# Score products of the later twenty tiles as two 64-row products, one per head of a pair, in place of one zero-padded 128-row product

## The chip, the cores and the metric

The kernel runs on one core of one Trainium2 chip. The metric is the device time of a run in microseconds. Engines: PE is TensorE's matmul side, PEld its weight loads, DVE is VectorE, ACT is ScalarE, POOL is GpSimd, SP is SyncE, which issues the DMAs.

## The reference, cut to what matters

```
batch 4, heads 8, sequence 768, head_dim 64, d_model 512, d_ff 1536
scores = q @ k^T / 8          # mask: heads 0, 2, 6 causal; the others 4 sinks + a window of 64
a      = softmax(scores)
x      = (a @ v), heads side by side            # (3072, 512)
out    = (silu(x @ w_gate) * (x @ w_val)) @ w_out
```

The result is compared with a float32 reference; the kernel multiplies in fp16 and accumulates in fp32.

Of the kernel before, what the change touches and what calls it, by code (L numbers as in the profile page):

```python
# [9 lines left out]
AF = mybir.ActivationFunctionType  # L10
# [102 lines left out]
def kernel(  # L113
# [13 lines left out]
    nc = tc.nc  # L127
# [29 lines left out]
    scale = 1.0 / (D ** 0.5)  # L157
# [18 lines left out]
    def buf(ring, shape, dt, name):  # L176
        return pools[ring].tile(shape, dt, name=name, tag=ring)
# [23 lines left out]
    def pe(d):  # L201
# [13 lines left out]
        out=ident, in_=ident, compare_op=ALU.not_equal, fill=1.0,  # L215
# [13 lines left out]
    OWN, DIAG, FAR, BAND0 = range(4)  # L229

    m0 = const.tile([128, 8, 128], FH, name="m0")
    m1 = const.tile([128, 4, 128], FH, name="m1")
    m2 = const.tile([128, 5, 128], FH, name="m2")
# [29 lines left out]

    def mask_fill(x):
        ps = mask_ps[0]
        for dst, src in ((m2[:, 0:1], OWN), (m2[:, 1:4], DIAG), (m2[:, 4:5], FAR),
                         (m1[:, 0:2], OWN), (m1[:, 2:4], FAR),
                         (m0[:, 0:4], BAND0), (m0[:, 4:6], DIAG), (m0[:, 6:7], BAND0),
                         (m0[:, 7:8], DIAG))[5 * x:5 + 5 * x]:
            nc.vector.tensor_scalar(  # L270
                out=dst, in0=ps[:, src].unsqueeze(1).to_broadcast([128, dst.shape[1], 128]),
                scalar1=-1.0 / OFF, op0=ALU.mult, scalar2=1.0, op1=ALU.add)
# [6 lines left out]
    qT = [const.tile([128, 2, 4, 2, 128], FH, name=f"qT{n}") for n in range(2)]  # L279
# [20 lines left out]
    def warm(n=40):  # L300
# [3 lines left out]
        for _ in range(n):  # L304
# [6 lines left out]
                     after=[T_fill0]) for x in range(4)]  # L311
    T_mord = P.add("mord", [pe(0.216)], -0.5, mask_order, deps=[T_masks], takes=["tr"])
    T_fill = [P.add(f"mfill{x}", [dve(1.3 + 0.1 * x)], -0.4, (lambda x=x: mask_fill(x)),
                    deps=[T_mord]) for x in range(2)]
    P.uses(T_mord, "tr", *T_fill)
# [96 lines left out]
    LEAD = 4  # L412
# [100 lines left out]
    def plan(t):  # L513


        b, i = TILES[t]
        if i == 0:
            if t == 0:
                return [([(p, (0, 1), 2 * x, 0) for x, p in enumerate(ps)], 4, None)
                        for ps in ((2, 3), (0, 1))]  # L520
            return [([(p, (0, 1), 2 * x, 0) for x, p in enumerate((2, 3, 0, 1))], 8, m0)]
        if t == 1:
            return [([(p, (0, 1), 0, i), (p, (0, 1), 2, -1)], 4, None) for p in (2, 3)] + [
                ([(1, (0, 1), 0, i), (0, (0, 1), 2, i)], 4, None),
                ([(1, (0,), 0, -1), (1, (1,), 1, 0), (0, (0, 1), 2, 0)], 4, None)]
        us = [([(2, (0, 1), 0, i), (2, (0, 1), 2, -1), (3, (0, 1), 4, i), (3, (0, 1), 6, -1)],
               8, m1),
              ([(1, (0, 1), 0, i), (0, (0, 1), 2, i), (1, (0,), 4, -1), (1, (1,), 5, 0),
                (0, (0, 1), 6, 0)], 8, m2)]
        rest = [(0, (0, 1), kt) for kt in range(1, i)] + [(1, (1,), kt) for kt in range(1, i)]  # L530
        unit, at = [], 0
        for p, hh, kt in rest:
            if at + len(hh) > 8:
                us.append((unit, at, None))
                unit, at = [], 0
            unit.append((p, hh, at, kt))
            at += len(hh)
        if unit:
            us.append((unit, at, None))
        return us  # L540

    def marks(t, u):

        if t >= LEAD:
            return []
        if t == 0:
            return [[(0, BAND0, 4)], [(0, DIAG, 2), (2, BAND0, 1), (3, DIAG, 1)]][u]
        if t == 1:
            return [[(0, OWN, 2), (2, FAR, 2)], [(0, OWN, 2), (2, FAR, 2)],
                    [(0, OWN, 1), (1, DIAG, 3)], [(0, FAR, 1)]][u]  # L550
        if TILES[t][1] == 0:
            return [(0, BAND0, 4), (4, DIAG, 2), (6, BAND0, 1), (7, DIAG, 1)]
        if u == 0:
            return [(0, OWN, 2), (2, FAR, 2), (4, OWN, 2), (6, FAR, 2)]
        return [(0, OWN, 1), (1, DIAG, 3), (4, FAR, 1)]

    def block(t, p, kt):

        b, i = TILES[t]
        if kt < 0 and i > 1:  # L560
            return k2[b % 2][:, p, i - 2, :]
        kt = max(kt, 0)
        return kT[b % 2][:, p, kt * 128:(kt + 1) * 128]

    def value(t, h, kt):
        b, i = TILES[t]
        if kt < 0 and i > 1:
            return v2[b % 2][:, i - 2, h, 0:65]
        return vt[b % 2][:, max(kt, 0), h, 0:65]

    whole_sc, es, av_blocks = {}, {}, {}

    def score_ring(t, u):
        return "gv" if t < 2 and u % 3 else "sc"

    def scores(t, u, unit):
        if t < 2:
            sc = [buf(score_ring(t, u), [128, 4, 128], FP, "sc")]
            whole_sc[t, u] = sc[0]
        else:  # L580
            sc = whole_sc[t, u] = buf("sc", [128, 8, 128], FP, "sc")
            sc = [sc[:, 0:4], sc[:, 4:8]]
        half = slice(t % 2 * 64, t % 2 * 64 + 64)
        terms = [(c, n, perm, nat[:, m].unsqueeze(1).to_broadcast([128, n, 128]))
                 for c, m, n in marks(t, u)]
        terms += [(c, len(hh), block(t, p, kt), qT[t // 2 % 2][:, hh[0]:hh[-1] + 1, p, :, half])
                  for p, hh, c, kt in unit[0]]
        for c, n, weights, moving in terms:
            first, last = True, True
            if t < LEAD:  # L590

                in_bank = [x for x in terms if x[0] // 4 == c // 4]
                first, last = moving is in_bank[0][3], moving is in_bank[-1][3]
            nc.tensor.matmul(  # L594
                sc[c // 4][:, c % 4:c % 4 + n, :], weights, moving, start=first, stop=last)

    def exps(t, u, unit):
        e = es[t, u] = buf("e", [128, 8, 128], FH, "e")
        for p, hh, c, kt in unit[0]:
            for n, s_ in enumerate(hh):  # L600
                h = PAIRS[p][s_]
                av_blocks.setdefault((t, h), []).append((e[:, c + n, :], value(t, h, kt)))
        n = unit[1]
        nc.scalar.activation(  # L604
            out=e[:, 0:n], in_=whole_sc.pop((t, u))[:, 0:n], func=AF.Exp, scale=scale)

    def mask(task, t, u, m):
        ev, mm = es[t, u][:, 0:m.shape[1]], m
        if m is m1:
            ev = es[t, u].rearrange("p (g n) q -> p g (n q)", g=2)  # L610
            mm = m.rearrange("p n q -> p (n q)").unsqueeze(1).to_broadcast([128, 2, 512])
        ENG[task().way[0]].tensor_tensor(out=ev, in0=ev, in1=mm, op=ALU.mult)  # L612
# [162 lines left out]
    def tasks_of_tile(t):  # L775
        b, i = TILES[t]
        pos = place(t)
        units = plan(t)
        n = t // 2
        k_deps = [x for kt in range(i // 2 + 1) for x in T_ev[QP.index((b, kt)), 2]]  # L780
# [8 lines left out]
        for u, unit in enumerate(units):  # L789
            mms, nb, m = unit  # L790
            sc = P.add(f"sc{t}.{u}", [pe(sum(0.056 if len(x[1]) == 1 else 0.109 for x in mms)
                                       + sum(x[2] * 0.056 for x in marks(t, u)))],
                       pos + 0.01 * u, (lambda t=t, u=u, unit=unit: scores(t, u, unit)),
                       deps=k_deps + (pk_deps if u < 2 else []) + ([T_masks] if t < LEAD else []), takes=[score_ring(t, u)], kind="",
                       grp=f"tile{t}", after=T_seq.get("sc", []))
            T_seq["sc"] = [sc]
            sc.nmm = len(mms) + len(marks(t, u))
            T_sc_of[b, i].append(sc)
            ex = P.add(f"ex{t}.{u}", [act(128 * nb)], pos + 0.01 * u,
                       (lambda t=t, u=u, unit=unit: exps(t, u, unit)), deps=[sc], takes=["e"],  # L800
                       grp=f"tile{t}", after=T_seq.get("ex", []))
            T_seq["ex"] = [ex]
# [3 lines left out]
            if m is not None and t >= LEAD:  # L806
                cell = []
                size = m.shape[1] * 128 * (2 if m is m1 else 1)
                ways = [pool(0.16 + size * 0.00192), both(0.08 + size * 0.00062)]
                ms.append(P.add(f"mask{t}.{u}", ways, pos + 0.01 * u,  # L810
                                (lambda cell=cell, t=t, u=u, m=m:
                                 mask(lambda: cell[0], t, u, m)),
                                deps=[ex] + T_fill, grp=f"tile{t}"))
                cell.extend(ms)
# [115 lines left out]
    for g in range(NG):  # L930
# [3 lines left out]
        for j in range(NJ):  # L934
# [5 lines left out]
            for c in parts:  # L940
                n = c[1] - c[0]
                mm = 4 * (n / 2400 + 0.0025)
# [99 lines left out]
```

## The kernel before: the parts that the change touches

The work is cut into 24 tiles of 128 queries. Heads go in pairs, and since a head has 64 dimensions, the pair's two heads fill the 128 partitions of `kT`: head 0 in rows 0 to 63, head 1 in rows 64 to 127. The queries `qT` hold, for each head of the pair, a block whose other 64 rows are zero. One product of the 128-row keys with both blocks side by side (256 columns) therefore gives both heads' scores at once, half of its multiplications being by zero.

```python
PAIRS = [(0, 2), (4, 6), (1, 3), (5, 7)]
kT = [const.tile([128, 4, S], FH, name=f"kT{n}") for n in range(2)]
qT = [const.tile([128, 2, 4, 2, 128], FH, name=f"qT{n}") for n in range(2)]
...
nc.vector.memset(qT[n][0:64, 1], 0.0)       # head 1's block: rows of head 0 are zero
nc.vector.memset(qT[n][64:128, 0], 0.0)
```

A *unit* is up to eight cells of 128 keys x 128 queries: two PSUM banks of four cells. `plan` lists the units of a tile; an entry is (pair, heads, first cell, key block). A unit's scores are followed by one exponential (ACT), a mask multiplication for some (POOL or DVE), and the value products.

```python
us = [([(2, (0, 1), 0, i), (2, (0, 1), 2, -1), (3, (0, 1), 4, i), (3, (0, 1), 6, -1)], 8, m1),
      ([(1, (0, 1), 0, i), (0, (0, 1), 2, i), (1, (0,), 4, -1), (1, (1,), 5, 0),
        (0, (0, 1), 6, 0)], 8, m2)]
...   # then the older key blocks, eight cells at a time

def scores(t, u, unit):
    ...
    terms += [(c, len(hh), block(t, p, kt), qT[t // 2 % 2][:, hh[0]:hh[-1] + 1, p, :, half])
              for p, hh, c, kt in unit[0]]
    for c, n, weights, moving in terms:
        ...
        nc.tensor.matmul(sc[c // 4][:, c % 4:c % 4 + n, :], weights, moving, start=first, stop=last)
```

The order of all work on each engine is fixed by a long string that the change leaves alone.

The softmax here doesn't subtract the row's maximum and nothing guards it: scores larger than these inputs give would overflow.

## Time and profile before

| | before |
|---|---|
| median of 3 runs | 268.32 us |
| lowest to highest | 268.29 to 268.49 us |
| profiled span | 266.5 us |
| matmuls, of them score products of the 54 units that change | 1984, 230 |
| busy: PE, ACT, DVE | 95%, 64%, 64% |

The lines on which most rests are shown in the prediction. How to read them: a digit of the busy rows is the busy share of one of 40 slices, in tenths. In a table of stretches the columns after the stretch and its length are the busy microseconds of PE, PEld, DVE, ACT and POOL, with counts. In the timeline the columns are start, duration, engine, line and operation, output from inputs, and how many were merged. A matmul's record is longer than its share of a stream (272 ns against 109 between starts in the prediction's timeline), so the distance from one start to the next, called *slot* here, is taken as what it costs in a stream. One more view of before is needed for the comparison: the weight loads ahead of and within a unit, from the timeline of PEld.

```profile
198.57 0.10 PEld L875 LDWEIGHTS <-wg_sb 128*128 128x128 f16 x1
198.79 0.10 PEld L594 LDWEIGHTS <-kT 128*128 128x128 f16 x1
199.00 0.10 PEld L594 LDWEIGHTS <-k 128*128 128x128 f16 x1
```

The first product of that unit starts at 199.00 (prediction, timeline). Its weights were loaded from 198.79, while the last gate product was still streaming: **each load runs one product ahead**.

### The profile page before, as it was taken

To read this page: it belongs to the slowest core of one execution; us is meant where nothing else is said; L and a number is where in the kernel's file an instruction comes from. 1 tells how busy PE (TensorE), PEld (TensorE's weight loads), DVE (VectorE), ACT (ScalarE), POOL (GpSimd) and SP (SyncE) were. 2 spreads that over 40 slices of the span, in tenths; PEclk is the share of its full clock that TensorE was granted. 3 is DMA by queue.
4 is the path that set the end of the run, shared out by engine and by line. 5 is a ranking of instruction groups with operands and counts; after the bars stand their busy time and mean duration, and the time that the engine had idled before them with its cause. 6 is when DMAs were issued, how large, how long until landed. Compare 5 with 4: busy or idle time off the path is not lost.

```text
span 266.5 us, 5265 instructions
## 1 busy us (share of the span) xinstructions
PE 254.4 (95%) x1984; PEld 146.4 (55%) x1984; DVE 171.6 (64%) x345; ACT 171.0 (64%) x283; POOL 92.3 (35%) x126
## 2 busy tenths in 40 slices
PE   7899689999999999999999999999999999999993
PEld 7777565566555555654555555545555654444441
DVE  7665678867476886549876455578446767466332
ACT  3799999999999874895696555665443643423000
POOL 8748866445358323388003230520122020000000
PEclk9999999999999999999999999999999999999999
DMA  7999999999899939956543911551231200101134
GB/s 189 305 333 333 305 328 383 317 246 305 259 292 217 230 85 299 213 108 127 118 92 60 159 39 43 117 100 23 63 76 21 57 7 17 39 2 41 39 89 109
DMA packets 75193, 41.23 MB, mean 155 GB/s; under 512 B 27552, under 2 KB 70560, under 8 KB 75168
## 3 DMA queue, kind: packets, MB, share of 16 engines
q1 hardware_dynamic: 75088, 40.78, 61.6%
q8 instruction: 15, 0.25, 0.4%
q10 hardware_dynamic: 80, 0.13, 0.2%
q14 instruction: 10, 0.08, 0.1%
HBM read 28.31 MB, written 6.29 MB: 130 GB/s over the span
## 4 chain that ended last, share of the span: by engine, by line
PE 71%; ACT 17%; DMA 3%; SPq 3%; issue 2%; DVE 1%; ACTq 0%
PE gv L875 40%; PE o_ps L904 20%; PE sc L594 7%; ACT e L604 5%; ACT v L183 4%; PE av L624 4%; DMA raw<-in_v_dram 3%; ACT vt L183 2%; ACT hq L183 2%; SPq L330 2%; ACT sig L881 2%; SPq L338 1%; ACT k L183 1%; PE tr L472 1%; ACT wo_sb L183 0%
## 5 line engine op out<-in xcount | busy, mean ns | idle before, releaser
L604 ACT ACTIVATE e<-sc 128x1024 f16<-128x1024 f32 (+4 forms) x71 | 62.2, 880 | 26.3 <-PE sc L594 25.9
L875 PE MATMUL gv<-xt,wv_sb 128*128 128x512 f16 (+1 forms) x304 | 70.8, 368 | 1.3 <-DVE sil L885 1.3
L904 PE MATMUL o_ps<-wo_sb,h 128*128 128x512 f16 x288 | 71.2, 379 | 0.1
L875 PE MATMUL gv<-xt,wg_sb 128*128 128x512 f16 (+1 forms) x304 | 70.6, 368 | 0.6 <-DVE xt L185 0.5
L885 DVE SCALAR_TENSOR_TENSOR sil<-sig,gv 128x512 f32<-128x512 f32 (+1 forms) x76 | 49.7, 656 | 31.7 <-ACT sig L881 31.1
L881 ACT ACTIVATE sig<-gv 128x512 f32<-128x512 f32 (+1 forms) x76 | 43.3, 574 | 36.5 <-PE gv L875 36.2
L892 DVE SCALAR_TENSOR_TENSOR h<-sil,gv 128x512 f16<-128x512 f32 (+1 forms) x76 | 48.7, 654 | 7.7 <-PE gv L875 7.0
L612 POOL TENSOR_TENSOR e<-e,m 128x640 f16<-128x640 f16 (+1 forms) x16 | 27.5, 1716 | 69.4 <-ACT e L604 54.3
L875 PEld LDWEIGHTS <-wv_sb 128*128 128x128 f16 x304 | 28.9, 98 | 29.0 <-issue 2.0
L875 PEld LDWEIGHTS <-wg_sb 128*128 128x128 f16 x304 | 28.9, 98 | 27.9 <-issue 1.6
L904 PEld LDWEIGHTS <-h 128*128 128x128 f16 x288 | 26.8, 98 | 26.1 <-issue 0.5
L594 PE MATMUL sc<-qT,kT 128*128 128x256 f16 (+1 forms) x228 | 35.6, 257 | 1.3 <-ACT e L604 1.2
L594 PEld LDWEIGHTS <-kT 128*128 128x128 f16 x228 | 20.5, 98 | 12.8 <-issue 2.3
L624 PEld LDWEIGHTS <-e 128*128 128x128 f16 x472 | 20.1, 97 | 8.2 <-ACT e L604 0.9
L185 POOL COPY v<-vt 32x528 f16<-32x528 f16 (+1 forms) x36 | 22.4, 621 | 4.6 <-ACT vt L183 2.5
L185 POOL CAST vt<-raw 64x512 f16<-64x512 f32 x23 | 15.8, 689 | 20.9 <-DMA raw<-in_v_dram 16.3
L624 PE MATMUL av<-vt,e 128*128 128x65 f16 x392 | 21.8, 193 | 0.5 <-ACT e L604 0.4
L641 DVE TENSOR_TENSOR xb<-av,rc 128x256 f16<-128x256 f32 x47 | 19.8, 424 | 1.6
L629 DVE RECIPROCAL rc<-av 128x4 f32<-128x4 f32 x48 | 8.5, 178 | 19.0 <-PE av L624 18.7
L183 ACT CAST hq<-raw 128x512 f16<-128x512 f32 x28 | 16.9, 617 | 4.4 <-DMA raw<-in_q_dram 3.6
L185 DVE COPY o_sb<-o_ps 128x512 f32<-128x512 f32 x14 | 9.6, 688 | 14.4 <-PE o_ps L904 14.4
L612 DVE TENSOR_TENSOR e<-e,m 128x1024 f16<-128x1024 f16 (+1 forms) x22 | 14.7, 670 | 6.3 <-ACT e L604 6.2
(62 smaller groups left out, 193.7 us busy)
## 6 DMA issues: line engine op xcount, KB each, us to landing
raw<-in_q_dram SPq DMA_DIRECT2D x12, 512.0 KB, 7.1
raw<-in_k_dram SPq DMA_DIRECT2D x12, 512.0 KB, 7.0
raw<-in_v_dram SPq DMA_DIRECT2D x12, 512.0 KB, 6.6
out_dram<-o_sb SPq DMA_DIRECT2D x47, 128.0 KB, 2.4
raw<-in_moe_w_gate_dram SPq DMA_DIRECT2D x6, 512.0 KB, 7.8
raw<-in_moe_w_val_dram SPq DMA_DIRECT2D x6, 512.0 KB, 8.4
raw<-in_moe_w_out_dram SPq DMA_DIRECT2D x6, 512.0 KB, 8.6
kT<-hq SPq DMA_TRANSPOSE x16, 2.4
```

The costliest lines, as they stand in the source:

```text
L183: nc.scalar.copy(out=dst, in_=src)
L185: ENG[task.way[0]].tensor_copy(out=dst, in_=src)
L594: nc.tensor.matmul(sc[c // 4][:, c % 4:c % 4 + n, :], weights, moving, start=first, stop=last)
L604: nc.scalar.activation(out=e[:, 0:n], in_=whole_sc.pop((t, u))[:, 0:n], func=AF.Exp, scale=scale)
L612: ENG[task().way[0]].tensor_tensor(out=ev, in0=ev, in1=mm, op=ALU.mult)
L624: nc.tensor.matmul(av[:, n, 0:65], ee, vv, start=(m == 0), stop=(m == len(bl) - 1))
L641: nc.vector.tensor_tensor(out=xbs[t][:, :, odd, :], in0=av[:, :, 0:64], in1=rc.to_broadcast([128, 4, 64]), op=ALU.mult)
L875: nc.tensor.matmul(ps, wsb[:, kk, j * 128:(j + 1) * 128], xt[:, kk, c[0]:c[1]], start=(kk == 0), stop=(kk == 3))
L881: nc.scalar.activation(out=sg[g, j, c], in_=gs[g, j, c], func=AF.Tanh, scale=0.5)
L885: nc.vector.scalar_tensor_tensor(out=sl[g, j, c], in0=sg.pop((g, j, c)), scalar=1.0, op0=ALU.add, in1=gs.pop((g, j, c)), op1=ALU.mult)
L892: nc.vector.scalar_tensor_tensor(out=hs[g, j][:, c[0]:c[1]], in0=sl.pop((g, j, c)), scalar=0.5, op0=ALU.mult, in1=vs.pop((g, j, c)), op1=A ...
L904: nc.tensor.matmul(o_open[g, tt], hs[g, j][:, tt * 128:(tt + 1) * 128], wo_sb[:, j, :], start=(j == 0), stop=(j == NJ - 1))
```

## The change

The intent: two heads' products with 64 rows each use different halves of the array's rows, so that they run beside each other, and 128 columns pass in place of 256. So that the two write different PSUM banks, the cells are laid out anew: head 0 in cells 0 to 3, head 1 in cells 4 to 7, and the masks follow. The first four tiles keep the old form, since their masks are added by 128-row products.

```diff
-        us = [([(2, (0, 1), 0, i), (2, (0, 1), 2, -1), (3, (0, 1), 4, i), (3, (0, 1), 6, -1)],
-               8, m1),
...
+        us = [([(2, (0, 1), (0, 4), i), (3, (0, 1), (1, 5), i), (2, (0, 1), (2, 6), -1),
+                (3, (0, 1), (3, 7), -1)], 8, m1),
+              ([(1, (0, 1), (1, 4), i), (0, (0, 1), (2, 5), i), (1, (0, 1), (3, 6), (-1, 0)),
+                (0, (0, 1), (0, 7), 0)], 8, m2)]
...   (the older key blocks and the masks likewise)
+        if isinstance(unit[0][0][2], tuple):
+
+            for entry in unit[0]:
+                for p, s_, c, kt in cells(entry):
+                    rows = slice(s_ * 64, s_ * 64 + 64)
+                    nc.tensor.matmul(
+                        sc[c // 4][:, c % 4, :], block(t, p, kt)[rows],
+                        qT[t // 2 % 2][rows, s_, p, :, half], start=True, stop=True)
+            return
```

54 units change, and none stands next to another in the order: 42 have four pairs, 4 have one pair and one single product, 4 have two pairs and two singles, 4 have three pairs and a single (one more one-head product of theirs moves to a small padded unit).

More of the change, by code (lines that the diff above doesn't have):

```diff
@@ L265, in mask_fill @@
         ps = mask_ps[0]
-        for dst, src in ((m2[:, 0:1], OWN), (m2[:, 1:4], DIAG), (m2[:, 4:5], FAR),
-                         (m1[:, 0:2], OWN), (m1[:, 2:4], FAR),
-                         (m0[:, 0:4], BAND0), (m0[:, 4:6], DIAG), (m0[:, 6:7], BAND0),
-                         (m0[:, 7:8], DIAG))[5 * x:5 + 5 * x]:
+        for dst, src in ((m2[:, 0:1], OWN), (m2[:, 1:2], DIAG), (m2[:, 2:3], FAR),
+                         (m2[:, 3:5], DIAG), (m1[:, 0:2], OWN), (m1[:, 2:4], FAR),
+                         (m0[:, 0:3], BAND0), (m0[:, 3:6], DIAG),
+                         (m0[:, 6:8], BAND0))[5 * x:5 + 5 * x]:
             nc.vector.tensor_scalar(
@@ L520, in plan @@
                         for ps in ((2, 3), (0, 1))]
-            return [([(p, (0, 1), 2 * x, 0) for x, p in enumerate((2, 3, 0, 1))], 8, m0)]
+            if t < LEAD:
+                return [([(p, (0, 1), 2 * x, 0) for x, p in enumerate((2, 3, 0, 1))], 8, m0)]
+            return [([(2, (0, 1), (0, 6), 0), (3, (0, 1), (1, 7), 0), (1, (0, 1), (2, 5), 0),
+                      (0, (0, 1), (3, 4), 0)], 8, m0)]
         if t == 1:
@@ L525, in plan, with cells, first_cell @@
                 ([(1, (0,), 0, -1), (1, (1,), 1, 0), (0, (0, 1), 2, 0)], 4, None)]
-        us = [([(2, (0, 1), 0, i), (2, (0, 1), 2, -1), (3, (0, 1), 4, i), (3, (0, 1), 6, -1)],
-               8, m1),
-              ([(1, (0, 1), 0, i), (0, (0, 1), 2, i), (1, (0,), 4, -1), (1, (1,), 5, 0),
-                (0, (0, 1), 6, 0)], 8, m2)]
-        rest = [(0, (0, 1), kt) for kt in range(1, i)] + [(1, (1,), kt) for kt in range(1, i)]
-        unit, at = [], 0
-        for p, hh, kt in rest:
-            if at + len(hh) > 8:
-                us.append((unit, at, None))
-                unit, at = [], 0
-            unit.append((p, hh, at, kt))
-            at += len(hh)
-        if unit:
-            us.append((unit, at, None))
-        return us
+        if t < LEAD:
+            us = [([(2, (0, 1), 0, i), (2, (0, 1), 2, -1), (3, (0, 1), 4, i), (3, (0, 1), 6, -1)],
+                   8, m1),
+                  ([(1, (0, 1), 0, i), (0, (0, 1), 2, i), (1, (0,), 4, -1), (1, (1,), 5, 0),
+                    (0, (0, 1), 6, 0)], 8, m2)]
+            return us
+        us = [([(2, (0, 1), (0, 4), i), (3, (0, 1), (1, 5), i), (2, (0, 1), (2, 6), -1),
+                (3, (0, 1), (3, 7), -1)], 8, m1),
+              ([(1, (0, 1), (1, 4), i), (0, (0, 1), (2, 5), i), (1, (0, 1), (3, 6), (-1, 0)),
+                (0, (0, 1), (0, 7), 0)], 8, m2)]
+        rest = list(range(1, i))
+        singles = [(1, (1,), kt) for kt in rest]
+        if rest:
+            free = 4 - len(rest)
+            unit = [(0, (0, 1), (3 - n, 4 + n), kt) for n, kt in enumerate(rest)]
+            unit += [(p, hh, (4 + len(rest) + n,), kt)
+                     for n, (p, hh, kt) in enumerate(singles[:free])]
+            us.append((unit, 2 * len(rest) + len(singles[:free]), None))
+            if singles[free:]:
+                us.append(([(p, hh, n, kt) for n, (p, hh, kt) in enumerate(singles[free:])],
+                           len(singles[free:]), None))
+        return us
+    def cells(entry):
+        p, hh, c, kt = entry
+        return [(p, s_, c[n] if isinstance(c, tuple) else c + n, kt[n] if isinstance(kt, tuple) else kt)
+                for n, s_ in enumerate(hh)]
+    def first_cell(unit):
+        return min(c for entry in unit[0] for _, _, c, _ in cells(entry))
     def marks(t, u):
@@ L599, in exps @@
         for p, hh, c, kt in unit[0]:
-            for n, s_ in enumerate(hh):
+            for _, s_, at, k_ in cells((p, hh, c, kt)):
                 h = PAIRS[p][s_]
-                av_blocks.setdefault((t, h), []).append((e[:, c + n, :], value(t, h, kt)))
-        n = unit[1]
+                av_blocks.setdefault((t, h), []).append((e[:, at, :], value(t, h, k_)))
+        n0 = first_cell(unit)
+        n1 = n0 + unit[1]
         nc.scalar.activation(
-            out=e[:, 0:n], in_=whole_sc.pop((t, u))[:, 0:n], func=AF.Exp, scale=scale)
+            out=e[:, n0:n1], in_=whole_sc.pop((t, u))[:, n0:n1], func=AF.Exp, scale=scale)
     def mask(task, t, u, m):
-        ev, mm = es[t, u][:, 0:m.shape[1]], m
+        n0 = 1 if m is m2 else 0
+        ev, mm = es[t, u][:, n0:n0 + m.shape[1]], m
         if m is m1:
```

## The prediction

> **What bounds the kernel now.** I read the page's busy digits first, then a table of busy time over two stretches, then the waits of PE, then single matmuls in the timeline. The busy digits of TensorE, of ScalarE and of the granted clock, in 40 slices of 6.7 us:
>
> ```profile
> PE   7899689999999999999999999999999999999993
> ...
> ACT  3799999999999874895696555665443643423000
> ...
> PEclk9999999999999999999999999999999999999999
> ```
>
> PE is full from slice 6 (about 40 us) to the end, at the full clock. ACT is full as well up to slice 12 (about 80 us), then falls away. So there are two stages, and I asked for the busy time of each engine in 40 to 78 us and 78 to 247 us (the last score product comes at 216 us, and from 247 us there are output products alone):
>
> ```profile
> 40.00:78.00 38.00, 36.55 (x326) 22.05 (x325) 26.24 (x52) 36.84 (x56) 18.25 (x23) 1.00 1.04 304
> 78.00:247.00 169.00, 168.65 (x1183) 89.66 (x1181) 113.89 (x220) 100.41 (x163) 44.86 (x51) 1.00 0.46 96
> ```
>
> The columns after the stretch and its length are PE, PEld, DVE, ACT, POOL. In the first stage PE and ACT are both at 96 to 97% and bind each other; in the second PE is at 99.8%, ACT at 59%, DVE at 67%. The waits of PE in that second stage are one line long:
>
> ```profile
> PE sc L594 <- ACT e L604: 0.4, 2, 0.3
> ```
>
> Busy time of PE overstates work, since matmuls overlap. So I took start-to-start distances. Four score products of two heads (256 columns), between two gate products:
>
> ```profile
> 198.78 0.38 PE L875 MATMUL gv<-xt,wg_sb 128*128 128x512 f16 x1
> 199.00 0.27 PE L594 MATMUL sc<-qT,kT 128*128 128x256 f16 x1
> 199.11 0.27 PE L594 MATMUL sc<-qT,k 128*128 128x256 f16 x1
> 199.22 0.27 PE L594 MATMUL sc<-qT,kT 128*128 128x256 f16 x1
> 199.33 0.27 PE L594 MATMUL sc<-qT,k 128*128 128x256 f16 x1
> 199.44 0.59 PE L875 MATMUL gv<-xt,wv_sb 128*128 128x512 f16 x2
> ```
>
> A score product takes a slot of 109 ns though its record lasts 272, and the step from gate to score and back costs nothing extra. Over the trace the median slot is 216 ns for 512 columns, 109 for 256, 56 for 128, and 29 for the 65 columns of a value product, each of which brings a weight load of its own. Added up, the distances after 80 us exceed these slots by only 2.2 us: from there **a nanosecond of PE slot is a nanosecond of kernel**, up or down. In 40 to 80 us they exceed them by 2.7 us, and ACT's exponentials, copies and casts stand right behind.
>
> **What the Trainium skill says.** "TensorEngine Tiling (Array Packing)", Tiling Modes, Key Properties: different tiles may run LdWeights and Matmul in parallel, but changing the tiling mode (not just the tile) drains the TensorE. It gives no time, and nothing in this trace shows one: every matmul of the kernel before has 128 rows. This is the number that decides. "TensorE: Matmul & The Clock Gate", Part 3, The mechanism: matmuls in different row groups start about 4 ns apart and run concurrently, and weight loads overlap in-flight matmuls where the row group differs. No run shows it yet. Same page, Part 1 ("Wait — 56ns, not 53.3ns?"): start to start is 55.6 ns at 128 columns and 215.7 at 512; the trace agrees (56 and 216). The tiling page, Gotcha 1: two row tiles must not write one PSUM bank at once. This is why the change moves the heads' cells into different banks and rearranges the masks.
>
> **The change part by part.** The order of instructions on each engine, compared between the two kernels, is the same in tasks and in waits; only the score products are replaced (PE goes from 1984 to 2158 matmuls, each with its weight load), and DVE fills the masks in 9 instructions as before, cut differently, in the first stage beside other work. The exponentials of all units together have as many elements; in the four tiles with i = 4 one block moves from a unit of 8 to the small one after it (896 and 256 columns in place of 1024 and 128), which costs nothing in sum. The mask products keep their sizes.
>
> *Removed.* 54 units change. By the trace they hold 174 products of two heads and 52 of one head: 174 x 109 + 52 x 56 = 21.9 us of PE slot.
>
> *Added.* 174 + 18 = 192 pairs of 64-row products (the 36 one-head products of the sink blocks become 18 pairs with different weights) and 16 one-head products that stay single (16 x 56 = 0.9 us). A pair needs two weight loads and two products. If they run together, the pair takes the larger of 56 + 4 = 60 ns (128 columns and the skill's offset) and 2 x 29 = 58 ns (twice the value product's slot, the closest thing in the trace to an issue limit for load and product). I take 60: 192 x 60 = 11.5 us. **Gross gain 21.9 - 11.5 - 0.9 = 9.5 us.** By stage: 39 of the units (128 two-head products, 13 sink pairs, 11 singles) start after 78 us. There 128 x 109 + 37 x 56 = 16.0 us become 141 x 60 + 11 x 56 = 9.1, so 6.9 us are saved where PE alone binds. The 15 units before 78 us save 2.6 us; with ACT at 97% beside it I let 1 us of that through. Useful gain 7.9 us.
>
> *The price.* Each unit is entered from a 128-row product and left for one: no two score units stand side by side in the order. That is 2 x 54 = 108 mode changes, 78 of them after 78 us and 30 before, of which ACT's waits may hide half: about 93 effective. Each costs the drain of what is in flight, and then a weight load that could not be fetched ahead. **Bounds from the trace.** A record lasts 163 ns longer than its slot at any size (379 - 216, 272 - 109, 219 - 56), so a drain to the modelled end would cost about 163, and a load starts about 27 ns ahead of its product: 190 ns at most. The cheapest is nothing beyond a few ns. The skill's TensorE page, Part 2 (step 4, DRAIN) has about 128 cycles for the wavefront to leave the array, which at 2.4 GHz is 53 ns; with 27 ns for the load, 80 ns. I choose 85 ns, an estimate: 93 x 0.085 = 7.9 us.
>
> *Sum.* -7.9 + 7.9 = 0: about 268.0 us. Break-even lies at 7.9 / 93 = 85 ns per change, in the middle of what I hold possible, so the change is a wager on one unmeasured number.
>
> **The rivals.** (1) *Mode changes nearly free* (under 30 ns). For: the engine already turns between shapes without loss, as the gate and score lines show. Against: the skill says it drains, and a load ahead of the change may be barred. Then -7.9 + 1 to 3 us: 261 to 263 us. (2) *Full drain* (150 to 190 ns): 93 x 0.17 = 15.8, net +8 us, about 276 us. For: the word "drains", and the 163 ns tail of every record. Against: the tail is modelled[...]. (3) *The pair doesn't overlap*, because 64-row loads are slower or serialize with the products: 192 x 112 = 21.5 us, no gain at all, and every change adds: 270 to 280 us. For: no run has shown it here. Against: the value products load 128 x 128 weights every 29 ns. (4) *ACT becomes the bound*: earlier scores bring earlier exponentials, but after 80 us ACT has 40% idle, so it can take only gains before that; this is counted in the 1 us.
>
> **Range and chances.** At 15 ns per change the time is 261.8, at 175 ns 276.7. I give 261.5 to 276 us as the range. Faster by over 2% (under 263.0 us) needs changes below about 30 ns and true overlap: 0.22. Slower by over 2% (above 273.7) needs above about 145 ns, or no overlap with over 60 ns: 0.26. The rest, 0.52, is within 2%.
>
> **What would show it.** In the profile after: two 64-row products of a pair starting a few ns apart, and pairs following each other every 60 ns, confirm the gain (a distance of 56 ns between all starts is rival 3). The gap from the last 128-row product's slot to a unit's first product, and from a unit's last product to the next gate product, beyond 0 in cases with no wait, is the price of a change; under 40 it is rival 1, over 150 rival 2. PE waits on ACT in 40 to 78 us should grow if ACT takes the gain there. A unit of four 109 ns slots, 436 ns from its first start to the next gate product's start, should last 240 plus the price. The prediction is wrong if mode changes cost far from 85 ns, or if a moved wait (a gate product on DVE, say) shows up after 80 us.

## More of the kernel before

All eight PSUM banks are in use: three for gate and value products of the feed-forward part, two for scores, one each for value products, transposes and outputs.

## The result, and the profile after

| | before | after |
|---|---|---|
| median (4 runs each, same chip) | 268.39 us | 269.47 us |
| lowest to highest | 268.29 to 268.49 | 269.46 to 269.91 |
| profiled span | 266.5 us | 268.1 us |
| matmuls | 1984 | 2158 |

The profiled run after was the slowest of its four (269.91 us), so its trace holds about 0.4 us more than the median. The ratio is 1.004, interval 1.0026 to 1.0055. A ratio here is the mean time of one kernel's fast runs over that of the other's fast runs of the same rounds, so it is not quite the ratio of the medians. The change makes the kernel 0.4% slower, which counts as the same at 2%. The prediction said 268.0 (261.5 to 276.0).

The busy digits of PE and of ACT after the change look as before:

```profile
PE   7999689999999999999999999999999999999993
...
ACT  3789999999999775795696555665444643423000
```

So do the two stages, in the table of stretches, the second being 2 us longer to hold the same work:

```profile
40.00:78.00 38.00, 36.66 (x364) 19.80 (x362) 26.49 (x52) 36.52 (x56) 18.19 (x23) 1.00 1.04 300
78.00:249.00 171.00, 169.91 (x1319) 81.94 (x1316) 115.08 (x222) 101.12 (x164) 44.57 (x52) 1.00 0.48 95
```

The bound hasn't moved. PE fills the second stage, ACT has as much room there as it had. The waits of PE in that stage have gained one short line:

```profile
PE sc L610 <- ACT e L635: 0.5, 2, 0.3
PE gv L907 <- DMA xt<-xb: 0.2, 1, 0.2
```

Now the same unit as in the prediction (there at 199.00 us), from the timeline of PE after the change:

```profile
199.88 0.81 PE L907 MATMUL gv<-xt,wg_sb 128*128 128x512 f16 x3
200.62 0.29 PE L610 MATMUL sc<-qT,kT 64*128 64x128 f16 x4
200.74 0.28 PE L610 MATMUL sc<-qT,k 64*128 64x128 f16 x4
200.95 0.61 PE L907 MATMUL gv<-xt,wv_sb 128*128 128x512 f16 x2
```

Four products start within 0.12 us of the first, and the next four begin then: eight products in the time that two needed before. In the trace a pair's two starts lie 3 to 4 ns apart, and the first products of successive pairs 56 ns (67 for the first to the second pair). **The overlap works fully.** But from the first score product to the next gate product it is 330 ns, where four pairs of 56 would be 224; and the first product starts at 200.62, although the last gate product (start 200.307 in the trace) had left its slot of 216 ns at 200.523. Nothing shows as idle for PE, because the records cover these gaps: their ends are modelled, and that of the last gate product lies at 200.686. PEld shows them, in the timeline of PEld after the change:

```profile
200.09 0.10 PEld L907 LDWEIGHTS <-wg_sb 128*128 128x128 f16 x1
200.61 0.12 PEld L610 LDWEIGHTS <-kT 64*128 64x128 f16 x4 [0.42 <-issue]
200.69 0.15 PEld L610 LDWEIGHTS <-k 64*128 64x128 f16 x4
200.94 0.33 PEld L907 LDWEIGHTS <-wv_sb 128*128 128x128 f16 x3
```

The unit's first load starts at 200.61, 4 ns ahead of its product, where before it was 210 ns ahead. It waits for nothing that the profile names ("issue"). On the way back the first 128-row load starts at 200.94, again 4 ns ahead of its product. Over all units the groups of the page show it too, before and after (the number behind the last bar is PEld's idle time ahead of these loads):

```profile
L594 PEld LDWEIGHTS <-kT 128*128 128x128 f16 x228 | 20.5, 98 | 12.8 <-issue 2.3
```

```profile
L610 PEld LDWEIGHTS <-kT 64*128 64x128 f16 x320 | 10.4, 94 | 20.2 <-issue 19.4
```

**The ledger of one visit.** I call it a visit when PE turns to 64-row products and back. From the starts in the trace, in all visits without another wait: 96 ns on the way in beyond the slot of the last 128-row product; 92 ns on the way out beyond the last pair's 56; the first 128-row product after it has a slot of 227 ns in place of 216 (39 in place of 29 for a value product), so 11 ns; the second pair comes 67 after the first in place of 56, 11 more; and the last pair ends its slot 3 late, by its own offset. Together **213 ns per visit, 106 per change of mode.** A unit of four pairs thus takes 4 x 56 + 213 = 437 ns (96 + 330 + 11 by the starts), where it took 436 to 440 in units without a wait. The full units are a draw. The small ones lose by the same count: one pair and a single 165 before, 96 + 218 + 11 = 325 after; two pairs and two singles 330 before, 437 after.

### The profile page after: what moved, and what is told of

Read it like the earlier page. It is cut to its first block, busy times and chain, and to the rows that moved or that the text cites. A ratio compares the mean times of both kernels' runs of the same rounds, so it can differ in the third digit from the quotient of the medians.

```text
span 268.1 us, 5612 instructions
## 1 busy us (share of the span) xinstructions
PE 255.6 (95%) x2158; PEld 137.0 (51%) x2158; DVE 172.6 (64%) x345; ACT 171.2 (64%) x283; POOL 91.6 (34%) x126
## 4 chain that ended last, share of the span: by engine, by line
PE 70%; ACT 14%; DMA 7%; SPq 4%; issue 3%; DVE 1%; POOL 1%; DVEq 0%; ACTq 0%
PE gv L907 42%; PE o_ps L936 18%; DMA raw<-in_v_dram 6%; PE sc L610 5%; PE av L656 4%; ACT e L635 4%; SPq L330 3%; ACT v L183 3%; ACT hq L183 2%; ACT vt L183 2%; DMA xt<-xb 1%; ACT sig L913 1%; SPq L338 1%; POOL vt L185 1%; ACT xt L183 1%
## 5 line engine op out<-in xcount | busy, mean ns | idle before, releaser
L635 ACT ACTIVATE e<-sc 128x1024 f16<-128x1024 f32 (+5 forms) x71 | 62.2, 880 | 25.5 <-PE sc L610 21.1
L907 PEld LDWEIGHTS <-wv_sb 128*128 128x128 f16 x304 | 28.0, 98 | 30.1 <-issue 1.9
L907 PEld LDWEIGHTS <-wg_sb 128*128 128x128 f16 x304 | 27.9, 98 | 29.7 <-issue 1.4
L936 PEld LDWEIGHTS <-h 128*128 128x128 f16 x288 | 26.0, 97 | 27.5 <-issue 0.5
L656 PEld LDWEIGHTS <-e 128*128 128x128 f16 x472 | 19.4, 97 | 9.1 <-ACT e L635 0.9
L185 POOL CAST vt<-raw 64x512 f16<-64x512 f32 x23 | 14.7, 638 | 19.9 <-DMA raw<-in_v_dram 15.2
L610 PEld LDWEIGHTS <-kT 64*128 64x128 f16 x320 | 10.4, 94 | 20.2 <-issue 19.4
L610 PE MATMUL sc<-qT,kT 64*128 64x128 f16 x320 | 19.2, 219 | 1.4 <-ACT e L635 1.2
```

The lines of the kernel that those rows point to most:

```text
L185: ENG[task.way[0]].tensor_copy(out=dst, in_=src)
L610: nc.tensor.matmul(sc[c // 4][:, c % 4, :], block(t, p, kt)[rows], qT[t // 2 % 2][rows, s_, p, :, half], start=True, stop=True)
L635: nc.scalar.activation(out=e[:, n0:n1], in_=whole_sc.pop((t, u))[:, n0:n1], func=AF.Exp, scale=scale)
L656: nc.tensor.matmul(av[:, n, 0:65], ee, vv, start=(m == 0), stop=(m == len(bl) - 1))
L907: nc.tensor.matmul(ps, wsb[:, kk, j * 128:(j + 1) * 128], xt[:, kk, c[0]:c[1]], start=(kk == 0), stop=(kk == 3))
L936: nc.tensor.matmul(o_open[g, tt], hs[g, j][:, tt * 128:(tt + 1) * 128], wo_sb[:, j, :], start=(j == 0), stop=(j == NJ - 1))
```

## The experiments

All results are recorded as correct, that of e9 too, though its edit gives both heads of a pair the first head's scores; e9 is used for its times alone. The extra runs of before on their chips had medians of 268.3, 268.7 and 268.5 us. The start of the kernel shifts its traces by up to 0.3 us from one execution to the next (0.2 us of that lay ahead of the first 64-row product in the trace of after), so differences below that are not read from single traces.

### The changed kernel again (e1_after_again)

No edit.

> The changed kernel once more, beside the others of this job. Ledger of PE slots from the two traces: 42 units of eight products gain 10 to 14 ns each (-0.5 us), 4 units of three products lose 150 (+0.6), 4 of six lose 96 (+0.4), 4 of seven gain 13 and the two products left over lose 56 (+0.2): +0.65 us in all. If the ledger is the whole story: 0.6 to 0.7 us over the kernel before; if waits elsewhere add to it, the 1.1 us of the first measurement again, ratio 1.004.

Measured: 269.54 us (5 runs, 269.0 to 269.94), ratio 1.004 (1.0028 to 1.0053). The first result stands. The expected ledger was too low, because I had left out the slower first product after a visit: 54 x 11 ns = 0.6 us. With it the ledger is +1.25 us if nothing is hidden in waits; +1.2 was measured. That the two agree so closely is in part chance, as the next run shows: some of the price is hidden, and another wait adds about as much.

### Full units only (e2_full_units_only)

```diff
+        if 1 < i < 5:
+            rest = ...          # the padded form and cells of before for the small units
+            return us
```

> Only the 42 units with four pairs are issued as 64-row pairs; the small units of the tiles with i = 2, 3, 4 go back to padded products and their old cells. Theory (price of 94 ns per change of mode against 53 ns saved per pair, PE the bound): 42 x -12 ns = -0.5 us, 0.2% below the kernel before. Rival (the split as such, its banks, masks or earlier exponentials, makes the loss): still above the kernel before, 268.8 or more.

Measured: 268.84 us (5 runs), ratio 1.0018 (1.0004 to 1.0032). This is better than the change, as the small units lose no more, but it is not below the kernel before. **My expectation was wrong by the 11 ns again**: with it a full unit gains nothing, so about 0 was due. The remaining 0.5 us sits at one place. The starts of all other products, compared with before, are 0.2 us *earlier* up to 144 us and 0.3 us later from 152 us on; between lies a wait that before doesn't have, in the waits of PE from 140 to 160 us:

```profile
PE gv L918 <- DMA xt<-xb: 0.4, 1, 0.4
```

A tile's normalized values go through a transposing DMA of 4.1 us here, and the gate product that needs them has no slack. The changed kernel's first profile has this wait for 0.2 us, e4 for 0.3; before, e1 and e3 have none on record. But the record of the product ahead covers most of the gap. The starts show it, from the timelines of before and of after:

```profile
150.33 1.02 PE L904 MATMUL o_ps<-wo_sb,h 128*128 128x512 f16 x4
151.19 2.75 PE L875 MATMUL gv<-xt,wg_sb 128*128 128x512 f16 x12
```

```profile
151.13 1.02 PE L936 MATMUL o_ps<-wo_sb,h 128*128 128x512 f16 x4
152.40 2.75 PE L907 MATMUL gv<-xt,wg_sb 128*128 128x512 f16 x12 [0.25 <-DMA xt<-xb]
```

Four slots of 216 ns end at 151.19 and 151.99. The gap is 1 ns in before, 411 in the changed kernel, 279 in e1, 589 in e2, 198 in e3 and 436 in e4. The transpose landed 3.5 us after its issue in before, 3.8 to 4.1 us in these five. Whether the new cells, small shifts of the issue order or chance in the DMA decide it, these runs do not tell (in e6, which has the old cells, the transpose ahead of this one takes 4.0 us).

### The new cells, padded products (e3_padded_new_cells)

```diff
-                        sc[c // 4][:, c % 4, :], block(t, p, kt)[rows],
-                        qT[t // 2 % 2][rows, s_, p, :, half], start=True, stop=True)
+                        sc[c // 4][:, c % 4, :], block(t, p, kt),
+                        qT[t // 2 % 2][:, s_, p, :, half], start=True, stop=True)
```

> Cells, masks, units and number of products (402) as in the changed kernel, but each product over all 128 rows, zero-padded, with 128 columns: no change of mode, no overlap. Theory: 400 x 56 in place of 174 x 109 + 52 x 56 and the same banks, so +0.5 us over the kernel before in slots (402 score products at 56 ns, the 5 extra left-over ones included). Rival (the new cells and masks cost something themselves): over +1.2 us.

Measured: 268.89 us (5 runs), ratio 1.0018 (1.0006 to 1.0031). (The 54 units hold 400 products; the expectation's 402 is a slip.) In the trace a full unit takes 446 to 447 ns (8 x 56) and is entered and left without a gap. The rival, that cells or masks cost something themselves, falls but for the gap of 198 ns at 151 us named above, which stays open: splitting alone costs about what eight slots of 56 cost beyond four of 109 (0.5 us by the expectation's sum). The thought that the gaps of the changed kernel come from the number of loads falls too.

### The heads apart in the order (e4_heads_apart)

```diff
-            for entry in unit[0]:
-                for p, s_, c, kt in cells(entry):
+            for want in range(2):
+                for p, s_, c, kt in [x for entry in unit[0] for x in cells(entry) if x[1] == want]:
```

> The same 64-row products, but in each unit all of the first head's ahead of all of the second's, so that only one pair can overlap in place of up to four; changes of mode stay. Theory: a full unit takes 3 x 53 = 160 ns more, 42 units 6.7 us, the small ones 0.5 us: 276 to 277 us. Rival (the overlap is worth little, or row tiles overlap in any order): 270 us.

Measured: 269.93 us (4 runs), ratio 1.0056. **A miss**: 0.4 us over the change, not 7. The unit at 200.8 us, as its products stand in the program:

```
gate | kT kT k k   (head 0)   | kT kT k k   (head 1)   | value
```

and as they started, from the timeline of PE:

```profile
200.80 0.30 PE L610 MATMUL sc<-qT,kT 64*128 64x128 f16 x4
200.93 0.28 PE L610 MATMUL sc<-qT,k 64*128 64x128 f16 x4
```

All four `kT` products started ahead of all four `k` products, so head 1's first two, the fifth and sixth of the program, were taken ahead of head 0's last two, the third and fourth. All 32 full units of this trace whose names can tell show such an order (in 16 of them the only `k` product, third in the program, starts fifth). From the second pair on the starts alternate by 13 and 43 ns, and a full unit takes 340 ns in place of 330. So the order of starts isn't the program's across the two row groups. My way of undoing the overlap did not undo it, and the run told nothing on the worth of it. The last run does.

### One more product per unit, 128 rows or 64 (e5_one_128row_extra, e6_one_64row_extra)

Both start from the kernel before, and put a product whose cells the unit then writes over at the head of the same 54 units:

```diff
+            nc.tensor.matmul(sc[0][:, 0, :], block(t, 0, 0), qT[t // 2 % 2][:, 0, 0, :, half], ...)         # e5
+            nc.tensor.matmul(sc[0][:, 0, :], block(t, 0, 0)[0:64], qT[t // 2 % 2][0:64, 0, 0, :, half], ...)  # e6
```

> The kernel before, with one more padded 128-row product of 128 columns at the head of each of the 54 units (its cells are written over by the unit). Theory (after 40 us a nanosecond of PE slot is a nanosecond of the kernel): 54 x 56 = +3.0 us, less what ACT hides before 78 us: 270.5 to 271.4. If PE had slack: less than 1 us.

> The same, but the extra product has 64 rows: one visit to the 64-row mode per unit, with nothing gained by it. Theory: 96 ns on the way in, 56 for the product, 92 on the way out, 244 x 54 = +13.2 us, less what ACT hides before 78 us: 279 to 281.6. The difference to the run with the 128-row product, over 108 changes of mode, is the price of one: 80 to 95 ns. Rival (the gaps seen in the changed kernel come from something else, its banks or its waits): like the 128-row product, 271.

Measured: 270.50 us (ratio 1.0073) and 279.31 us (ratio 1.0401), against 268.68 for before. The second has only the number of rows of one product per unit in other form, half as many multiplications, and costs 8.8 us more. Over 108 changes that is 82 ns each on average, waits hiding a part. A unit of e6 in the timeline of PE:

```profile
207.71 0.81 PE L881 MATMUL gv<-xt,wg_sb 128*128 128x512 f16 x3
208.45 0.23 PE L592 MATMUL sc<-qT,kT 64*128 64x128 f16 x1
208.61 0.28 PE L600 MATMUL sc<-qT,kT 128*128 128x256 f16 x1
208.73 0.27 PE L600 MATMUL sc<-qT,k 128*128 128x256 f16 x1
```

The lone product holds PE until 208.61, and the first product after it takes 120 ns where its sisters take 109. Units of the second stage lasted 265 ns longer than before by the starts, 209 beyond the product's own 56: **the price of a visit, without any of the change's banks, cells, masks or pairs.** These runs also show how ACT hides it. In e6 the 15 units before 78 us cost 15 x 265 = 4.0 us, and at 80 us the kernel is 1.9 us late: about half. In the second stage 39 x 265 = 10.3 us are paid and 9.1 are lost by the starts: the kernel before has gaps of 1.6 us between the slots there (the largest, 0.2 to 0.35 us each, ahead of score products; two are on record as waits for ACT), and e6 has only 0.4 left. In e5 1.8 of 39 x 56 = 2.2 us are lost.

### Both kernels with each unit's products issued twice (e7_before_doubled, e8_after_doubled)

```diff
-        for c, n, weights, moving in terms:
+        for c, n, weights, moving in terms + (terms if full(t, unit) else []):     # e7
-            for entry in unit[0]:
+            for entry in unit[0] + unit[0]:                                        # e8
```

> The kernel before with the products of the same 54 units issued twice in a row into the same cells (same results): +174 x 109 + 52 x 56 = +21.9 us, 288 to 290 us.

> The changed kernel with each unit's products issued twice within one visit: +192 x 56 + 16 x 56 = +11.6 us over the changed kernel, 280 to 281 us, since the changes of mode are paid once per visit. Theory (fixed price per visit): 3% below the doubled kernel before. Rival (the price grows with the products in a visit): no better than the doubled kernel before, 290.

Measured: 287.29 us and 277.76 us. Both are misses, by 0.7 and 2.2 us: again part of the added time went into waits (at 78 us e8 is 1.1 us behind the changed kernel by the starts, while its units up to there hold 56 more slots of 56 ns, 3.1 us). The comparison of the two holds: with twice the score products per visit the 64-row form is 3.3% faster than the padded form doubled alike. A unit of e8, in the timeline of PE:

```profile
206.29 0.81 PE L907 MATMUL gv<-xt,wg_sb 128*128 128x512 f16 x3
207.04 0.29 PE L610 MATMUL sc<-qT,kT 64*128 64x128 f16 x4
207.16 0.28 PE L610 MATMUL sc<-qT,k 64*128 64x128 f16 x4
207.27 0.28 PE L610 MATMUL sc<-qT,kT 64*128 64x128 f16 x4
207.38 0.28 PE L610 MATMUL sc<-qT,k 64*128 64x128 f16 x4
207.59 0.39 PE L907 MATMUL gv<-xt,wv_sb 128*128 128x512 f16 x1
```

Sixteen products from 207.04 to 207.59: 553 ns, with 96 on the way in and 11 after it 660 in all, where the doubled padded unit takes 873. Eight slots of 56 ns make 448, so the price is 212 ns, as for four pairs. So **the price is per visit, not per product**, and the rival falls.

### Both products of a pair in one row group (e9_one_row_group, wrong result)

```diff
-                    rows = slice(s_ * 64, s_ * 64 + 64)
+                    rows = slice(0, 64)
-                        qT[t // 2 % 2][rows, s_, p, :, half], start=True, stop=True)
+                        qT[t // 2 % 2][rows, 0, p, :, half], start=True, stop=True)
```

> The changed kernel with both products of every pair in the same 64 rows (the first head's; a wrong result on purpose): same number of products, loads, banks and changes of mode, but no two row groups that could overlap. Theory (two row groups run beside each other, 53 ns saved per pair): a full unit takes 4 x 53 = 212 ns more, 42 units 8.9 us, the small ones 1.3 us, less what ACT hides before 78 us: 278 to 280 us. Rival (the overlap is not between row groups, since putting the heads apart in the order cost nothing): 270 us.

Measured: 276.89 us (4 runs), ratio 1.0312: 7.4 us over the changed kernel, which was measured in another job. In the timeline of PE:

```profile
206.19 0.40 PE L610 MATMUL sc<-qT,kT 64*128 64x128 f16 x4
206.43 0.38 PE L610 MATMUL sc<-qT,k 64*128 64x128 f16 x4
206.74 0.39 PE L907 MATMUL gv<-xt,wv_sb 128*128 128x512 f16 x1
```

Eight products in 550 ns, a slot of 56 each, in place of 330. The full unit lost 220 ns, as expected. The total came out somewhat below 278, as again some of it lies behind ACT and other waits. So the overlap of two row groups is worth about 7 us of this kernel's time, and it is real in the change.

## Why the prediction was right

The time lay 1.5 us above the predicted one and well inside its range. (Its own sum, no change, would be 268.3, the time before; it wrote 268.0.) The range was wide, 85 ns was chosen between bounds of a few and 190 ns, and the two main terms both came out larger than foretold and partly cancel: so near a hit is in part luck. By its steps:

- **PE slots are the bound after 80 us.** Right in the main. The second stage is still full (169.91 of 171.00), and PE waits 0.7 us in it. But a nanosecond of slot was not a whole nanosecond of kernel there: 1.8 of 2.2 us came through in e5, 9.1 of 10.3 in e6.
- **The gain.** The prediction took 60 ns for a pair, from 56 + 4 and 2 x 29. Measured: 56, since the 4 ns between the two starts don't add up from pair to pair. In the prediction's own sum the second stage saves 16.0 - (141 + 11) x 0.056 = 7.5 us in place of 6.9, and the useful gain is 8.5 in place of 7.9. (Its 52 one-head products leave out the four that move to padded units; e7 adds 230 matmuls, 174 + 56. The four cancel in the sum.)
- **The price of a change of mode.** The prediction estimated 85 ns as 53 (wavefront) + 27 (load) and a little over. Measured: 106. Both parts were off, in opposite directions. From the end of the last slot to the load it was 91 ns (200.523 to 200.614, the load's start in the trace), not 53; but the load comes only 4 ns ahead of its product, not 27. And there are two items of 11 ns each which the prediction did not have: a slower first product after the visit, and a slower second pair.
- **Half of the price before 78 us hidden.** Right by e6 (1.9 of 4.0 us).
- **The sum with measured terms.** -8.5 + 93 x 0.106 = +1.4 us, against +1.1 and +1.2 measured. Two things that it leaves out nearly cancel. Start by start, the first trace after falls back 0.86 us against before from 78 us on, and e1's 0.73; 0.41 and 0.28 of that is the gap ahead of the gate product at 152 us, so about 0.45 us is left for the visits, where -7.5 + 78 x 0.106 makes 0.8. The rest of their price there went into waits that before has too. What came before 78 us stays an estimate.
- **The rivals.** Free changes and a full drain of 190 ns are both refuted by the gaps and by e6; pairs that don't overlap by the starts and by e9; ACT as the new bound by the second stretch. The sign foretold for ACT, longer PE waits from 40 to 78 us, did not show: the waits on the exponential there were 1.0 us before and are 0.7 after, since there was no net gain for ACT to take.

What the prediction had not looked at is the size of the units. At 53 ns saved per pair (109 - 56) and 213 ns per visit, break-even is 213 / 53 = 4.0 pairs. The full units have four. The small ones, with one to three, lose 0.64 us (one pair) and 0.43 us (two pairs) of the ledger's 1.25; the wait at 152 us is the other large item.

No run beats the kernel before. What might, by e8, is a visit of eight pairs: 660 ns in place of 873 for two padded units. That needs two more PSUM banks at the time, and all eight are in use, so it would need another schedule. It was not tried.

## What to carry to other kernels

Row tiling of a 64-deep contraction halved the streaming time fully here, but each visit to the tiled mode among 128-row products cost a fixed price (213 ns), so count the pairs per visit, not in all: here zero padding was the better form below four pairs of 128 columns. Batch the small products into few visits before going over, and look for the price in start-to-start distances and in the idle time of the weight loads, because the busy time of PE does not show it.

## What the Trainium skill lacked or had wrong

- "TensorEngine Tiling (Array Packing)", Tiling Modes, Key Properties: it says that a change of mode drains the TensorE, but gives no time. The runs show 96 ns in, 92 out, 11 on the first product after, 11 on the second pair and 3 on the last: 213 ns per visit (209 in e6, with one product in a visit).
- The same page does not say whether weight loads of the next mode are fetched ahead across the change. In these traces they were not: the load started 4 ns ahead of its product, 210 ns without a change of mode.
- "TensorE: Matmul & The Clock Gate", Part 3, The mechanism: it calls matmuls strictly in program order in start and end. In e4 products of one row group started ahead of earlier ones of the other (four `kT`, then four `k`, where the program has them mixed). Its 4 ns between the starts of a pair holds (3 to 4 ns); for a row of pairs it gives no figure, and the runs show 56 ns per pair, with no 4 ns added for each.
